# Seven half-size products for eight in the first large matmul, from the fifth block of nine on

## The chip, the cores and the metric

The kernel runs on one core of a Trainium2 chip. A core has a matrix engine (TensorE, PE in the profile; its weight loads are listed apart as PEld), a vector engine (DVE), a scalar engine (ACT), a general engine (POOL), a sync engine (SP) that here issues nearly all transfers, and 16 DMA engines. Each engine works through its own list of instructions in order and waits where an instruction needs a result of another engine. The metric is the device time of one execution in microseconds.

## The reference

```
q_s = softmax(q, axis=-1);  k_s = softmax(k, axis=2)          # q, k, v: 8 x 8 x 576 x 64
kv  = einsum('bhsd,bhse->bhde', k_s, v)
x   = einsum('bhsd,bhde->bhse', q_s, kv)  -> 4608 tokens x 512
h   = x @ w_in                                                # 512 x 2048
g   = s * maximum(h, 0)**2 + b                                # s, b: one number each
out = g @ w_out                                               # 2048 x 512
```

A linear attention gives 4608 tokens of 512 features. Two large products follow, with a squared ReLU, a scale `s` and an offset `b` between them. All arrays are float32.

## The kernel before, in words

**Blocks and steps.** The tokens form nine blocks of 512. Blocks 0 to 7 hold the first 512 tokens of one batch each; the ninth, block 8, collects the 64 left over from each batch. The 2048 hidden features are cut into 16 chunks of 128, so that a block has 16 steps and the program 144 (`step`, L738). Weights and tokens are kept split into a high and a low part, and each product is made as high x high, high x low and low x high, summed in PSUM. One step is 12 matmuls of 128 x 512 for `h` (four parts of the 512 features, three each, L726) and 12 of 128 x 512 for the output (four groups of 128 tokens, three each, L814). All of w_in and w_out stay in SBUF, in tiles called `w`, after they have been converted in block 0.

**Between the two products** stand four instructions per step: ACT takes the ReLU from PSUM (`r`, L770), DVE squares and scales (L785), ACT adds `b` and rounds to the high part `gh` (L787), DVE forms the low part `gl` (L789). Of the eight PSUM banks `h` has one and the output (`acc`) four; one called `sm` and a pair called `big` serve the attention.

**The attention of block n+1** is worked on while block n is in the two products: loads of q, k and v, maxima by way of DRAM, exponentials, a turn of q by way of DRAM (`turned`, then `qT`), the small products `kv` (L299) and `xp`, `xq` (L676), and the sum `y` of their halves (ACT L682, DVE L686). The result is rounded into the high and low parts of `x` (ACT L690, DVE L694). POOL does two large instructions for each pair of heads (L575, L592).

**What sets the order.** Every piece of work is an `Op` with an engine, a planned cost, a due number, the results it needs, and the buffers it takes and frees. A small planner (`Order.run`) goes through all streams and writes out, engine by engine, a fixed order: of the pieces that could start at nearly the same planned moment, the one with the lowest due number. On the chip each engine keeps that order.

**At a block's exit** ACT and DVE copy one half of `acc` each to SBUF and SP stores it (`leave`, L825, L828). The last block leaves in four quarters (`leave_last`, L840).

## Time and profile before

| what | value |
|---|---|
| median of 3 runs (range) | 872.04 us (871.01 to 872.32) |
| span of the profiled execution | 869.5 us |
| PE busy | 851.7 us, 98% |
| weight loads busy | 701.9 us, 81% |
| DVE busy | 570.8 us, 66% |
| ACT busy | 416.3 us, 48% |
| POOL busy | 91.4 us, 11% |
| bytes moved by DMA | 79.44 MB |

The profile is of one execution. Its span runs from the first to the last instruction; the run times are 2.5 us longer in the median (872.04 - 869.5), which is what lies around the span. Times in the timeline are microseconds from the span's start; "mean ns" is the mean duration of one instruction of a group. A matmul's recorded duration overlaps that of the next one, so its rate is read from the distance between starts. Block 1 begins at about 132 us, block 4 at about 410 us, block 7 at about 687 us; blocks 1 to 6 take some 92 us each, the attention's small products included.

### The profile page before, as it was taken

How to read it: one execution, taken by the hardware profiler on the slowest of the kernel's cores; microseconds unless marked ns; L12 is line 12 of the kernel's file. 1: busy time of each engine (PE TensorE's matmuls, PEld its weight loads, DVE VectorE, ACT ScalarE, POOL GpSimd, SP SyncE). 2: the span in 40 equal slices, each digit the busy share in tenths (PEclk: the TensorE clock that was granted, in tenths of full speed). 3: DMA queues.
4: the chain of work that ended last, by engine and by line, in shares of the span. 5: the costliest groups of instructions: out<-in, count | busy, mean ns of one | idle time of the engine just before them, and what ended most of it. 6: DMA issues, size and time to landing. Idle time of an engine off the chain costs nothing.

```text
span 869.5 us, 11637 instructions
## 1 busy us (share of the span) xinstructions
PE 851.7 (98%) x4367; PEld 701.9 (81%) x4367; DVE 570.8 (66%) x916; ACT 416.3 (48%) x694; POOL 91.4 (11%) x117
## 2 busy tenths in 40 slices
PE   7799999999999999999999999999999999999997
PEld 6578887888888888888888888888888888888886
DVE  6999997596877777686677658785855322232222
ACT  5989864544554545353545354444544322222222
POOL 1000002021102111111021202020200010000000
PEclk9999999999999999999999999999999999999999
DMA  8994134424433334342433242432311000000001
GB/s 232 308 378 136 26 86 118 127 74 97 137 82 89 83 119 100 90 92 78 130 89 83 89 130 75 96 89 82 77 61 52 33 16 1 1 30 19 1 1 48
DMA packets 109991, 79.44 MB, mean 91 GB/s; under 512 B 60656, under 2 KB 103664, under 8 KB 109808
## 3 DMA queue, kind: packets, MB, share of 16 engines
q1 hardware_dynamic: 108496, 77.60, 31.8%
q10 hardware_dynamic: 1440, 1.12, 0.4%
q8 instruction: 34, 0.56, 0.3%
q14 instruction: 21, 0.17, 0.1%
HBM read 60.29 MB, written 18.40 MB: 91 GB/s over the span
## 4 chain that ended last, share of the span: by engine, by line
PE 92%; DVE 4%; DMA 1%; SPq 1%; issue 1%; ACT 0%; ACTq 0%; DVEq 0%
PE acc L814 44%; PE h L726 44%; PE kv L299 2%; PE xp L676 1%; PE xq L676 1%; DMA k<-in_k_dram 1%; DVE low L216 1%; DMA st<-in_moe_w_in_dram 0%; DVE st L213 0%; PE xp L440 0%; DVE w L223 0%; DMA v<-in_v_dram 0%; SPq L288 0%; DVE low L206 0%; DVE st L211 0%
## 5 line engine op out<-in xcount | busy, mean ns | idle before, releaser
L726 PE MATMUL h<-x,w 128*128 128x512 f32 x1728 | 420.2, 391 | 2.4 <-ACT r L770 1.2
L726 PEld LDWEIGHTS h<-x,w 128*128 128x128 f32 x1728 | 322.7, 188 | 71.6 <-ACT r L770 1.9
L814 PE MATMUL acc<-w,gh 128*128 128x512 f32 x1152 | 357.8, 392 | 0.8 <-ACT gh L780 0.8
L814 PEld LDWEIGHTS acc<-w,gh 128*128 128x128 f32 x1152 | 214.0, 188 | 45.6 <-ACT gh L780 1.2
L785 DVE SCALAR_TENSOR_TENSOR r<-r,sb 128x512 f32<-128x512 f32 x135 | 106.1, 786 | 190.1 <-ACT r L770 189.7
L814 PE MATMUL acc<-w,gl 128*128 128x512 f32 x576 | 224.5, 390 | 0.6 <-DVE gl L782 0.6
L770 ACT ACTIVATE r<-h 128x512 f32<-128x512 f32 x143 | 85.5, 598 | 277.3 <-PE h L726 264.9
L789 DVE SCALAR_TENSOR_TENSOR gl<-r,sb,gh 128x512 fp32r<-128x512 f32 x135 | 104.5, 774 | 56.5 <-ACT gh L787 55.2
L787 ACT ACTIVATE gh<-r,sb 128x512 fp32r<-128x512 f32 x135 | 97.7, 724 | 84.8 <-DVE r L785 84.4
L814 PEld LDWEIGHTS acc<-w,gl 128*128 128x128 f32 x576 | 108.1, 188 | 23.8 <-DVE gl L782 1.1
L575 POOL TENSOR_TENSOR q<-q,qm 128x640 f32<-128x640 f32 x24 | 33.7, 1406 | 161.4 <-DVE qm L573 161.4
L592 POOL TENSOR_TENSOR qe<-qe,qr 128x640 f32<-128x640 f32 x24 | 32.3, 1347 | 65.8 <-DVE qr L588 43.7
L682 ACT COPY y<-xp 64x320 f32<-64x320 f32 x48 | 20.2, 420 | 13.8 <-PE xp L676 13.4
L686 DVE TENSOR_TENSOR y<-xp,y 64x320 f32<-64x320 f32 x48 | 23.5, 489 | 3.4 <-ACT y L682 2.5
L562 ACT ACTIVATE k<-k 128x640 f32<-128x640 f32 x24 | 17.7, 737 | 15.1 <-DVE k L524 12.3
L596 DVE STREAM_TRANSPOSE q<-qe 128x640 f32<-128x640 f32 x24 | 19.9, 831 | 5.2 <-POOL qe L592 5.2
L299 PEld LDWEIGHTS kv<-v,k 128*64 128x64 f32 x600 | 18.7, 137 | 5.1 <-issue 4.4
L656 POOL TENSOR_TENSOR spare<-kvf,spare 128x256 fp32r<-128x256 f32 x12 | 10.1, 844 | 118.6 <-issue 112.8
L613 DVE TENSOR_TENSOR qhl<-qT,qhl 64x640 fp32r<-64x640 f32 x24 | 20.6, 860 | 1.1 <-ACT qhl L610 0.4
L686 DVE TENSOR_TENSOR y<-xq,y 64x256 f32<-64x256 f32 x48 | 20.3, 422 | 1.0
L299 PE MATMUL kv<-v,k 128*64 128x65 f32 (+1 forms) x600 | 20.8, 224 | 0.0
L200 ACT ACTIVATE low<-st 128x1024 int32<-128x1024 uint32 (+1 forms) x17 | 18.9, 1111 | 3.2 <-DVE w L223 1.9
(124 smaller groups left out, 619.6 us busy)
## 6 DMA issues: line engine op xcount, KB each, us to landing
st<-in_moe_w_in_dram SPq DMA_DIRECT2D x16, 512.0 KB, 8.7
st<-in_moe_w_out_dram SPq DMA_DIRECT2D x16, 512.0 KB, 9.1
out_dram<-o SPq DMA_DIRECT2D x16, 512.0 KB, 2.7
turned<-q SPq DMA_DIRECT2D x24, 320.0 KB, 2.3
qT<-turned SPq DMA_DIRECT2D x48, 160.0 KB, 3.0
k<-in_k_dram SPq DMA_DIRECT2D x14, 512.0 KB, 4.2
q<-in_q_dram SPq DMA_DIRECT2D x14, 512.0 KB, 5.3
v<-in_v_dram SPq DMA_DIRECT2D x56, 128.0 KB, 4.8
```

The source lines that it names most:

```text
L299: nc.tensor.matmul(kv[h * D:(h + 1) * D, i], kt[:, i, h, n], vt[:, 2 * i + h, n], start=(n == 0), stop=(n == NT - 1))
L575: nc.gpsimd.tensor_tensor(out=qt, in0=qt, in1=bc(qm, [P, 2, NT, D]), op=ALU.subtract)
L592: nc.gpsimd.tensor_tensor(out=qe_, in0=qe_, in1=qr, op=ALU.mult)
L613: nc.vector.tensor_tensor(out=t[half[1 - h], h], in0=qT[half[h]], in1=t[half[h], h].bitcast(F32), op=ALU.subtract)
L682: nc.scalar.copy(y[half[h], at], parts[h][a][half[1 - h]])
L686: nc.vector.tensor_tensor(out=y[half[h], at], in0=parts[h][a][half[h]], in1=y[half[h], at], op=ALU.add)
L726: nc.tensor.matmul(hp_, w[:, j, c, :], x[:, c, :], start=(c == 0 and i == 0), stop=(c == NP - 1 and i == 2))
L770: nc.scalar.activation(r, hp_, AF.Relu)
L785: nc.vector.scalar_tensor_tensor(out=r, in0=r, scalar=s_col, in1=r, op0=ALU.mult, op1=ALU.mult)
L787: nc.scalar.activation(gh, r, AF.Identity, bias=b_col)
L789: nc.vector.scalar_tensor_tensor(out=gl, in0=r, scalar=b_col, in1=gh.bitcast(F32), op0=ALU.add, op1=ALU.subtract)
L814: nc.tensor.matmul(acc[blk, j // 2][:, j % 2], g[:, js], w_, start=(f == 0 and i == 0), stop=(f == NFC - 1 and i == 2))
```

## The change

From block 4 on (`PLAIN = 4`), the first product is made for two chunks of hidden features at a time (a pair; 40 pairs in five blocks). Weights of a pair form a 2 x 2 array of halves: two chunks (A1., A2.) by two halves of the 512 input features. The tokens form one too: two halves of the features by two halves of 256 tokens (B11, B12, B21, B22). The product of the two arrays takes eight half-size products; here it is made of seven, of sums and differences:

```
S1 = A21 + A22   S3 = A11 - A21   S2 = S1 - A11   S4 = A12 - S2
T1 = B12 - B11   T3 = B22 - B12   T2 = B22 - T1   T4 = B21 - T2
order:  P0 = A11 B11   P1 = S1 T1   P2 = A22 T4   P3 = S2 T2   P4 = S3 T3   P5 = A12 B21   P6 = S4 B22
second chunk row:  P2 + u3,  P1 + u3      with u1 = P0, u2 = P0 + P3, u3 = P0 + P3 + P4
first chunk row:   P5 + u1,  P1 + P6 + u2
```

- Each half-size product is six matmuls of 128 x 256 (L976). All seven are summed in two PSUM banks, `hset` (four quarters of 256 columns); P0, P3 and P4 follow one another in one quarter, and ACT copies the quarter out after each (u1, u2, u3, L1024). So P3 waits for the copy u1, P4 for u2, P5 for u3, P6 for the DVE sum of the second row (L1027), and the next pair's P0 for the DVE sum of the first row (L1038).
- The seven weight arrays of each pair are formed once, in blocks 1 to 3, from the converted w_in (`combine`: DVE and POOL sums, ACT and POOL splits), and stored in DRAM (14.7 MB written). In blocks 4 to 8 they are read back for every block, two products to a transfer of 512 KB, 140 transfers (`stream`, L912). The room comes from the w_in tiles, set free in block 3.
- The tokens' arrays T1 to T4 and their splits are formed per block when `x` is ready (`prepare`), for block 4 to 8.
- Between the products there are now, per pair, for one row ReLU, square and rounding on ACT and the low part on DVE; for the other one DVE instruction for ReLU and square (L997), rounding on ACT, low part on POOL (L1014).
- In blocks 4 to 7 `s` and `b` enter at the exit: out = s (r^2 w_out) + b (column sums of w_out). POOL adds up the 16 tiles of w_out in 30 additions, one pair of PE matmuls spreads the sums (`column_sums`), and both halves leave by way of DVE (L1173). Block 8 keeps `s` and `b` in the rows.
- The small products for blocks 5 to 7 take the one bank `h` in two turns in place of `big`, which `hset` holds.
- The planner gets other due numbers, and a cost added to DVE work while POOL works.

In the diff, cut:

```diff
+    DUE_S = (15.5, 13.5, 61.0, 51.0, 93.0, 76.0, 121.0, 150.5)
+    DUE_B = (33.5, 38.5, 39.5, 55.0, 37.5, 41.0, 57.5, 91.0, 95.0, 88.0, 115.0, 85.5)
+    PLAIN, FOLD = 4, 4
+    HP, OPS = NFC // 2, 7
+    KEPT = 6
...
+        else:
             for h in range(2):
+                yield Op("PE", 0.29, due - NFC, needs=needs, take=["h", "sm"], gives=[f"xp{u}"] * h, late=WAIT)
...
+    ORDER = ("A11", "S1", "A22", "S2", "S3", "A12", "S4")
+    WITH = {"A11": "B11", "S1": "T1", "A22": "T4", "S2": "T2", "S3": "T3", "A12": "B21", "S4": "B22"}
...
+    def stream(m):
...
+        yield Op("SP", 0.65, NFC * blk + 2 * uses[0][0] + DUE_ST, needs=needs, take=["pc", "ahead"], kb=512, gives=[f"s{m}"])
+        W[m] = slot()
+        nc.sync.dma_start(W[m].bitcast(F32), ws[n].rearrange("p o l e -> p o (l e)"))
...
+    def products(p):
...
+        before = {
+            0: [f"row1 {p - 1}", f"o{t - 3} {NQ - 1}"], 1: [], 2: [], 3: [f"u1 {p}"], 4: [f"u2 {p}"], 5: [f"u3 {p}"], 6: [f"row2 {p}"]
+        }
...
+        where = (1, 3, 2, 1, 1, 0, 3)
+        for k, name in enumerate(ORDER):
...
+            out_ = hset[0][:, where[k] * M:(where[k] + 1) * M]
+            w = W[m][:, j].rearrange("p (l c e) -> p l c e", l=2, c=2)
+            n = 0
+            for kt in range(2):
+                xs = x_of(blk, x, kt)
+                for a, b_ in ((0, 0), (0, 1), (1, 0)):
+                    nc.tensor.matmul(out_, w[:, a, kt], xs[:, b_], start=k < 2 and n == 0, stop=n == 5, skip_group_check=True)
+                    n += 1
...
+    def rows_a(p):
...
+        for n, k in enumerate((0, 3, 4)):
+            yield Op("ACT", 0.38, due, needs=[f"P{k} {p}"], late=LAG, near=SOON[0], gives=[f"u{n + 1} {p}"])
+            V, U = raw["V"][p % 2], raw["U"]
+            nc.scalar.copy(U if n == 2 else V[:, n * M:(n + 1) * M], hset[0][:, M:2 * M])
+        yield Op("DVE", 0.74, due, needs=[f"P2 {p}"], late=LAG, near=SOON[1], take=["r"], gives=[f"row2 {p}"])
...
-            + [step(t) for t in range(NSTEP)]
+            + [step(t) for t in range(PLAIN * NFC)]
+            + [late_(), column_sums()] + [g(i) for g in (keep_parts, combine) for i in range(HP)] + [release(f) for f in range(NFC)] + [streams()]
+            + [g(p) for p in range(NPAIR) for g in (products, rows_a, rows_b)] + [outputs(t) for t in range(PLAIN * NFC, NSTEP)]
```

**PE, two steps late in block 8.** Before, one `h` chunk of twelve matmuls and the twelve of the output of the chunk before:

```order
L726 MATMUL h_140_7075<-x_8_6142,w_12_1022 128x512 x12
L814 MATMUL acc_8_0_6734<-w_11_984,gh_139_7060 128x512 x2
L814 MATMUL acc_8_0_6734<-w_11_984,gl_139_7061 128x512
L814 MATMUL acc_8_0_6734<-w_11_984,gh_139_7060 128x512 x2
L814 MATMUL acc_8_0_6734<-w_11_984,gl_139_7061 128x512
L814 MATMUL acc_8_2_6746<-w_11_984,gh_139_7060 128x512 x2
L814 MATMUL acc_8_2_6746<-w_11_984,gl_139_7061 128x512
L814 MATMUL acc_8_2_6746<-w_11_984,gh_139_7060 128x512 x2
L814 MATMUL acc_8_2_6746<-w_11_984,gl_139_7061 128x512
L726 MATMUL h_141_7107<-x_8_6142,w_13_1085 128x512 x12
```

Now, in the last pair: P0 and P1 (two rows each), P2 (the row of six), P3, six output matmuls, P4, six output matmuls; P5, P6 and the rest of the output follow. The `w_`, `slots` names are tiles that now hold token arrays, streamed weights or `g`:

```order
L976 MATMUL hset_4051<-w_0_293,w_8_782 128x256 x3
L976 MATMUL hset_4051<-w_1_480,w_8_782 128x256 x3
L976 MATMUL hset_4051<-w_0_293,slots_4029 128x256 x3
L976 MATMUL hset_4051<-w_1_480,slots_4029 128x256 x3
L976 MATMUL hset_4051<-w_6_668,slots_4029 128x256 x6
L976 MATMUL hset_4051<-w_9_861,w_15_1280 128x256 x3
L976 MATMUL hset_4051<-w_10_887,w_15_1280 128x256 x3
L1157 MATMUL acc_8_0_7723<-w_12_1022,w_13_1085 128x512 x6
L976 MATMUL hset_4051<-w_9_861,w_15_1280 128x256 x3
L976 MATMUL hset_4051<-w_10_887,w_15_1280 128x256 x3
L1157 MATMUL acc_8_2_7738<-w_12_1022,w_13_1085 128x512 x6
```

Six output matmuls stand between P3 and P4 and again between P4 and P5; between P0 and P3 stand only P1 and P2.

**DVE in block 5.** Before, at the turn from block 4 to 5, the two instructions per step stand among those of the attention (`qhl`, `spare`, `z`):

```order
L785 SCALAR_TENSOR_TENSOR r_80_4635<-r_80_4635,sb_88 128x512
L613 TENSOR_TENSOR spare_1379<-qT_25_4574,spare_1379 64x640 x2
L825 COPY o_4_1_4663<-acc_4_2_3913 128x1024
L789 SCALAR_TENSOR_TENSOR gl_80_4637<-r_80_4635,sb_88,gh_80_4636 128x512
L785 SCALAR_TENSOR_TENSOR r_81_4694<-r_81_4694,sb_88 128x512
```

Now, in the middle of block 5, the two row sums (L1027, L1038) for which PE waits stand among them:

```order
L544 TENSOR_TENSOR k0_90<-k0_90,mb_13_5401 128x640 x2
L1027 TENSOR_TENSOR row_88_5562<-hset_4051,late_3196 128x2x4x64
L659 TENSOR_SCALAR z_13_5595<-kv_13_5564 128x2
L660 RECIPROCAL z_13_5595<-z_13_5595 128x2
L666 TENSOR_TENSOR kvf1_84<-kv_13_5564,z_13_5595 64x2x64 x4
L1038 TENSOR_TENSOR late_3196<-hset_4051,late_3196 128x2x4x64
L1014 TENSOR_TENSOR gl_1_4033<-row_88_5562,gh_1_4032 128x512
L997 SCALAR_TENSOR_TENSOR late_3196<-late_3196 128x512
L632 TENSOR_TENSOR qhl_1378<-qT_26_5484,qhl_1378 64x640 x2
```

Before, no DVE result stood between one `h` chunk's matmuls and the next one's but by way of the output; now P6 and the next P0 each wait for one.

**SP in block 5.** Before, the queue held the attention's transfers and the output; now the streamed weights (L912) stand among them, in one queue:

```order
L912 DMA w_14_1144<-ws_9_1863 128x1024
L912 DMA w_8_782<-ws_10_2082 128x1024
L1180 DMA out_0_dram<-o_4_0_5162 128x1024
L1180 DMA out_0_dram<-o_4_1_5173 128x1024
L912 DMA w_11_984<-ws_11_2101 128x1024
L912 DMA slots_4029<-ws_12_2400 128x1024
L912 DMA w_15_1280<-ws_13_2084 128x1024
L529 DMA maxima_13_5302<-top_13_5284 128x4x2
L912 DMA w_1_480<-ws_14_2331 128x1024
L912 DMA w_2_516<-ws_15_2343 128x1024
L618 DMA turned_26_5390<-q0_91 128x2x320
```

Each streamed transfer waits for a free tile, and the attention's transfers behind it in the queue wait with it.

395 lines of the change are left out of this document (337 added, 58 removed).

## The prediction

> **What bounds the kernel now.** First the page: engine shares, and the chain that ended last.
>
> ```profile
> span 869.5 us, 11637 instructions
> PE 851.7 (98%) x4367; PEld 701.9 (81%) x4367; DVE 570.8 (66%) x916; ACT 416.3 (48%) x694; POOL 91.4 (11%) x117
> GB/s 232 308 378 136 26 86 118 127 74 97 137 82 89 83 119 100 90 92 78 130 89 83 89 130 75 96 89 82 77 61 52 33 16 1 1 30 19 1 1 48
> PE 92%; DVE 4%; DMA 1%; SPq 1%; issue 1%; ACT 0%; ACTq 0%; DVEq 0%
> ```
>
> PE is busy for 98% of the span and makes up 92% of the chain (the GB/s row, in 40 slices, serves the transfers below). Averages hide stages, so next the view by windows (us, then busy time of PE, weight loads, DVE, ACT, POOL, then granted clock, DMA share, GB/s): the start, two windows in the blocks that the change touches while attention is still made, and one after it.
>
> ```profile
> 0.00:30.00 30.00, 22.28 (x207) 18.58 (x208) 22.11 (x41) 20.28 (x45) 3.80 (x21) 1.00 0.93 272
> 430.00:520.00 90.00, 90.00 (x472) 74.59 (x471) 64.08 (x109) 41.82 (x73) 13.91 (x14) 1.00 0.34 93
> 520.00:610.00 90.00, 90.00 (x470) 74.52 (x469) 64.92 (x110) 41.70 (x72) 13.62 (x14) 1.00 0.32 89
> 700.00:780.00 80.00, 80.00 (x355) 66.24 (x354) 22.28 (x29) 21.92 (x34) 4.06 (x3) 1.00 0.00 1
> ```
>
> From block 4 on PE has no idle time at full clock, and DVE, ACT and DMA have room. So every microsecond of PE work taken out there comes off the end, unless a new wait takes its place. What the PE work is, by groups (count, busy us, mean ns):
>
> ```profile
> L726 PE MATMUL h<-x,w 128*128 128x512 f32 x1728 | 420.2, 391 | 2.4 <-ACT r L770 1.2
> L814 PE MATMUL acc<-w,gh 128*128 128x512 f32 x1152 | 357.8, 392 | 0.8 <-ACT gh L780 0.8
> L814 PE MATMUL acc<-w,gl 128*128 128x512 f32 x576 | 224.5, 390 | 0.6 <-DVE gl L782 0.6
> ```
>
> Durations overlap here, so rates must come from starts, in the timeline (start, duration, engine, line, count). PE's rows around the small products of block 4, and around the last `h` chunk:
>
> ```profile
> 468.24 0.31 PE L676 MATMUL xp<-qhl,spare 128*128 128x320 f32 x1
> 468.39 0.28 PE L676 MATMUL xq<-qhl,spare 128*128 128x256 f32 x1
> 468.51 0.31 PE L676 MATMUL xp<-qhl,spare 128*128 128x320 f32 x1
> 468.65 0.28 PE L676 MATMUL xq<-qhl,spare 128*128 128x256 f32 x1
> 468.77 0.39 PE L814 MATMUL acc<-w,gh 128*128 128x512 f32 x1
> ...
> 856.06 2.88 PE L726 MATMUL h<-x,w 128*128 128x512 f32 x12
> 858.78 0.39 PE L814 MATMUL acc<-w,gh 128*128 128x512 f32 x1
> ```
>
> Twelve full-size matmuls take 858.78 - 856.06 = 2.72 us, 0.2267 us each. Half-size ones (256 columns, each with its own weight load) take 468.51 - 468.39 = 0.12 and 468.77 - 468.65 = 0.12. Finer: the four take 0.53 us for 1152 columns; with 0.2267 for 512 that makes 0.42 ns a column and 0.011 us a matmul, so 0.119 us for 256. A half costs 52% of a whole.
>
> **The change, part by part.** *PE.* Removed: blocks 4 to 8 had 5 x 16 x 12 = 960 full-size `h` matmuls, 960 x 0.2267 = 217.6 us. Added: 40 pairs x 7 x 6 = 1680 half-size ones, 1680 x 0.119 = 199.9 us. Net **-17.7 us**, 0.44 per pair. The rounding of the rows allows 0.116 to 0.121: -22.7 to -14.3. In the trace half-size matmuls alternate with longer ones, in the change 42 weight loads come with 42 half-size matmuls nearly in a row. Can loads keep up? The rows of the transposes, which load 128 x 128 each and stream only 128 columns:
>
> ```profile
> 29.77 0.92 PE L440 MATMUL xp<-early,kvf 128*128 128x256 f32 x3
> 30.52 0.71 PE L430 MATMUL qT<-ident,qe 128*128 128x128 f32 x5
> ...
> L430 PE MATMUL qT<-ident,qe 128*128 128x128 f32 x40 | 5.7, 274 | 0.2 <-DVE qe L426 0.2
> ...
> L440 PE MATMUL xp<-early,kvf x32: 377/432/483, 19.9 to 134.8; 128*128 128x256 f32 x16, 128*128 128x320 f32 x16
> ```
>
> Five take 0.71 us, the last 0.274 of it: (0.71 - 0.27) / 4 = 0.11 us from load to load. That is under 0.119, so loads still hide, barely. The break-even is (217.6 - 1.8) / 1680 = 0.128 us per half-size matmul.
>
> *Column sums on PE.* Two plain float32 products of 512 columns. Of such products the first row above has three instructions in 30.52 - 29.77 = 0.75 us (one of 256 columns, two of 320), 0.84 ns a column. Each product is recorded twice (32 rows of L440 for 16 in the program), so two of 512 columns are 4 x 512 x 0.84 = 1.7; **+1.8 us** with the hand-over. The 30 POOL additions ahead of them have all of block 3.
>
> *The waits inside a pair* are the new risk. The rows that price them:
>
> ```profile
> 858.98 0.66 ACT L757 ACTIVATE r<-h 128x256 f32<-128x256 f32 x2 [3.30 <-PE h L726]
> 862.38 0.59 ACT L840 COPY last<-acc 128x512 f32<-128x512 f32 x1 [1.55 <-PE acc L814]
> 863.01 0.19 PEld L814 LDWEIGHTS acc<-w,gh 128*128 128x128 f32 x1 [0.42 <-ACT last L840]
> ...
> L682 ACT COPY y<-xq 64x256 f32<-64x256 f32 x48 | 17.6, 367 | 0.9
> L686 DVE TENSOR_TENSOR y<-xp,y 64x320 f32<-64x320 f32 x48 | 23.5, 489 | 3.4 <-ACT y L682 2.5
> L686 DVE TENSOR_TENSOR y<-xq,y 64x256 f32<-64x256 f32 x48 | 20.3, 422 | 1.0
> ```
>
> ACT started 0.20 us after PE went on to other work (858.98 against 858.78); PE started 0.04 after ACT's end (862.97 to 863.01). A quarter's copy is 0.37. So u1, u2, u3 take 0.20 + 0.37 + 0.04 = 0.61 us each. By PE's new order P0 to P3 is covered by P1 and P2 (12 x 0.119 = 1.43), P3 to P4 and P4 to P5 by six output matmuls (1.36). A row sum of 512 columns is an estimate from L686: 67 ns per 64 columns more, 0.69 us. P4 to P6 takes copy, sum and three hand-overs, 0.20 + 0.37 + 0.05 + 0.69 + 0.04 = 1.35, cover 1.36 + 0.71 = 2.07; P6 to the next P0 0.93, cover 2.72. With engines free nothing waits. In blocks 7 and 8 they are free: DVE 22.28 of 80 us.
>
> In blocks 4 to 6 foreign work stands in front. DVE: 64.08 per 90 us is 65.8 per block of 92.4; less 16 steps of L785 and L789, plus the new rows:
>
> ```profile
> L785 DVE SCALAR_TENSOR_TENSOR r<-r,sb 128x512 f32<-128x512 f32 x135 | 106.1, 786 | 190.1 <-ACT r L770 189.7
> L789 DVE SCALAR_TENSOR_TENSOR gl<-r,sb,gh 128x512 fp32r<-128x512 f32 x135 | 104.5, 774 | 56.5 <-ACT gh L787 55.2
> L782 DVE TENSOR_TENSOR gl<-r,gh 128x512 fp32r<-128x512 f32 x8 | 5.5, 692 | 2.2 <-ACT gh L780 2.2
> L770 ACT ACTIVATE r<-h 128x512 f32<-128x512 f32 x143 | 85.5, 598 | 277.3 <-PE h L726 264.9
> L787 ACT ACTIVATE gh<-r,sb 128x512 fp32r<-128x512 f32 x135 | 97.7, 724 | 84.8 <-DVE r L785 84.4
> L613 DVE TENSOR_TENSOR qhl<-qT,qhl 64x640 fp32r<-64x640 f32 x24 | 20.6, 860 | 1.1 <-ACT qhl L610 0.4
> L712 POOL TENSOR_TENSOR x<-xleft_all,x 128x512 fp32r<-128x512 f32 x4 | 5.4, 1338 | 72.5 <-ACT x L710 72.5
> L694 DVE TENSOR_TENSOR x<-y,x x24: 628/684/1752, 179.6 to 666.0; 128x512 fp32r<-128x512 f32 x24
> ```
>
> 65.8 - 25.0 = 40.8; plus 8 pairs x (2 x 0.69 + 0.786 + 0.692) = 22.9; plus token arrays (six of 0.42, five of 0.69, 6.0, less four L694 of 0.84, 3.4) 2.6; plus the exit's other half 1.2: 67.5 of a block of 88.9, 76% against 71%. So the engine is no bound, but one attention instruction (0.86, L613) in front of a row sum makes it 2.21 against a cover of 2.07; two make it 3.07. (An ACT instruction of 0.72 in front of u2 makes 1.33, still covered.) Below: nothing. Above: 0.8 us, one instruction too many, in each of 24 pairs, 19 us. I take 0.1 per pair, **+2.4 us**, near the lower end, since DVE is free a quarter of the time and one foreign instruction costs 0.14.
>
> *POOL* gets 8 low parts and three splits per block, 11 x 1.338 = 14.7 us, and DVE feels POOL: L694 takes 0.684 in the median and 1.752 at most. The Trainium skill ("SBUF — State Buffer", "SBUF: two separate sides") says of the port pair that DVE and GpSimd share that it is an exclusive lock, the loser waiting out the whole instruction. The 1.752 agrees; by it 14.7 us more would be lost to DVE per block, 82 of 88.9 us by my estimate.
>
> *Blocks 1 to 3* get the weight sums: DVE 16 x 0.69 + 16 x 0.42 = 17.8 us in 277, POOL 46 x 1.338 and 16 of half that, 72 us, the column sums included. There an `h` chunk's way to the output has 24 matmuls of cover (5.44 us) for 0.598 + 0.786 + 0.724 + 0.774 = 2.9 us and four hand-overs: nothing. *The end:* after the last P6 stand 24 output matmuls, 5.44 us, before chunk 15's; its row needs 0.93 + 0.79 + two ACT instructions like L787 (1.45) + POOL 1.34, 4.5. Nothing.
>
> *Transfers.* 28 x 0.524 = 14.7 MB per block of 88.9 us, 165 GB/s, beside 93: 258 GB/s. The first window had 272 at a share of 0.93, its third slice 378. Six transfers are held ahead, twelve products, over 15 us, against:
>
> ```profile
> st<-in_moe_w_in_dram SPq DMA_DIRECT2D x16, 512.0 KB, 8.7
> qT<-turned SPq DMA_DIRECT2D x48, 160.0 KB, 3.0
> ```
>
> The stream is covered even at 8.7 us. The attention's own round trips, behind it in SP's queue, may come later: 0 to 8 us in three blocks; I take none.
>
> **Sum.** 869.5 - 17.7 + 1.8 + 2.4 = 856.0 for a profiled span; the median of the runs lies 2.5 above the span: **858.5 us**.
>
> **Rivals.**
> *Attention comes late.* PE's list has 24 halves of `xp` and 6 `kv` for blocks 5 to 7 in it, each now needing `sm`, `h` and DRAM round trips. If the busier queue (3.0 to 8.7 us landing) delays 6 turns of q by what the cover doesn't hold, 6 x 1.3 = 8 us: 866.5. For: the share of 0.93 in the first window. Against: the 378 GB/s of the third slice, so 258 is no ceiling.
> *Row sums behind stretched attention work, slower than before.* Place: P6 and P0 in blocks 4 to 6. Price: a row sum behind one L613 (0.86) and one POOL stretch (1.752 - 0.684 = 1.07) needs 1.35 + 1.93 = 3.28 against 2.07, 1.2 us in each of 24 pairs, 29 us: 885. It decides from (17.7 - 1.8) / 24 = 0.66 us per pair. For: 76% on an engine that works in order. Against: the stretch is the extreme of 24.
> *A half-size matmul costs more than half.* If each had to show a part of its 0.188 us load and cost three quarters of a whole, 0.170 us, then 1680 x 0.170 = 285.6, +68 in place of -17.7: 944. Against: the 0.12 and the 0.11. The Trainium skill ("TensorE: Matmul & The Clock Gate", "Back-to-back issue gap") gives a sustained 81 ns for 128 columns and 131 for 512; by a line through these, an estimate, a half is three quarters of a whole. The trace's 0.2267 and 0.119 disagree with both.
> *No stalls at all* and 0.1175 per matmul: 853.
>
> **How the numbers follow.** Forecast 0.60, late attention 0.18, slower by row sums 0.08, dear half-size 0.02, no stalls 0.12. The first reaches from 855 to 862; with the two neighbours 852 to 868 holds some 85 in 100. A change under 0.2% can't be told from none: 870.3 to 873.8 counts as the same, chance 0.03; slower 0.09 (the two rivals less what falls short of the point, and the tail); faster 0.88.
>
> **What would show it.** `hset` matmuls 0.117 to 0.121 us from start to start, blocks 7 and 8 some 3.5 us shorter than 87 and PE without idle: the first term. Idle of PE before `hset` by DVE or ACT over 5 us in blocks 4 to 6: the row sums. Idle before `xp` or `kv` with the turn of q late: the transfers. I am wrong if `hset` matmuls stand 0.125 us or more apart, or if blocks 1 to 3 grow.

## The result and the profile after

The changed kernel takes **917.64 us** (median of 4 runs, 915.16 to 918.19) against 872.18 us (871.01 to 872.97): ratio 1.0515, 95% interval 1.05 to 1.0531. Forecast were 858.5 us, 852 to 868. It is slower by 45 us where 14 us less were forecast; of the two rivals on the slower side the row sums had 885 and the dear half-size matmuls 944. The profiled execution has a span of 913.4 us in a time of 915.16 (the lowest of the four); the ledger below is made on spans.

The page of the changed kernel: the span, the busy time of the engines, the shares of the chain that ended last (the work and waits followed back from the last instruction).

```profile
span 913.4 us, 13898 instructions
PE 863.1 (94%) x5091; PEld 725.4 (79%) x5091; DVE 641.1 (70%) x989; ACT 483.4 (53%) x881; POOL 246.0 (27%) x230
PE 71%; DVE 15%; issue 4%; ACT 4%; SPq 2%; DMA 2%; POOL 1%; DVEq 0%; ACTq 0%; POOLq 0%
```

PE fell from 98% to 94% of the span and from 92% to 71% of the chain; DVE's share of the chain rose from 4% to 15%. So PE now waits. Where, the windows tell, cut at the first `h` or `hset` matmul of each block (us, busy time of PE, weight loads, DVE, ACT, POOL, then granted clock, which is the share of TensorE's full rate that it had in that stretch, DMA share, GB/s). Before, blocks 1 to 3, and block 7:

```profile
131.90:225.60 93.70, 93.69 (x485) 77.34 (x485) 71.44 (x120) 47.20 (x81) 17.42 (x17) 1.00 0.37 95
225.60:318.00 92.40, 92.40 (x482) 76.59 (x481) 68.72 (x117) 43.88 (x77) 14.58 (x15) 1.00 0.38 105
318.00:410.30 92.30, 92.30 (x481) 76.52 (x480) 68.71 (x116) 44.66 (x78) 13.84 (x16) 1.00 0.37 96
...
687.40:774.50 87.10, 87.10 (x386) 72.11 (x385) 26.52 (x34) 24.12 (x37) 5.35 (x4) 1.00 0.03 13
```

After, blocks 1 to 7:

```profile
131.70:226.30 94.60, 94.03 (x485) 77.28 (x486) 73.56 (x120) 47.65 (x81) 26.53 (x25) 1.00 0.56 152
226.30:323.10 96.80, 93.87 (x483) 76.17 (x482) 88.08 (x139) 48.85 (x89) 40.66 (x35) 1.00 0.62 171
323.10:432.10 109.00, 98.93 (x482) 77.42 (x481) 101.81 (x132) 48.05 (x88) 70.16 (x51) 0.97 0.43 124
432.10:527.10 95.00, 90.98 (x618) 79.44 (x617) 69.14 (x120) 53.28 (x109) 26.69 (x24) 1.00 0.84 253
527.10:625.00 97.90, 92.87 (x626) 80.91 (x625) 70.17 (x119) 50.89 (x107) 27.45 (x25) 1.00 0.79 234
625.00:721.20 96.20, 92.46 (x625) 80.74 (x624) 60.69 (x103) 50.41 (x105) 23.70 (x22) 1.00 0.70 222
721.20:811.80 90.60, 86.91 (x529) 76.09 (x528) 30.34 (x45) 34.16 (x68) 14.19 (x12) 1.00 0.54 187
```

Two losses of different kinds stand in these rows. Block 3, which the change gives no new product, takes 109.0 us for 92.3, with DVE busy for 101.8 of them and POOL for 70.2. PE is idle for 10.1 us there; the other 6.6 are busy time, 98.9 for 92.3 us at nearly the same number of matmuls (482 and 481): ahead of a stop a matmul counts with its whole 0.39 us, where otherwise the next one starts after 0.2267. And block 7, where DVE is busy for 30 of 90 us and nothing of attention is left, takes 90.6 for 87.1 where 3.5 less were forecast: PE has 3.7 us idle there. What ended PE's idle times (us in total, times, longest):

```profile
PE hset L976 <- ACT late L1024: 18.6, 40, 1.0
PE acc L1157 <- DVE gl L1132: 6.1, 8, 1.9
...
PE hset L976 <- DVE row L1027: 1.4, 6, 0.6
```

The first row is the key to blocks 4 to 8: there are 40 pairs, and PE waits 40 times for ACT's copy of a quarter, once in every pair. The forecast had that copy covered.

The time from the first product of each block to that of the next, for all kernels of this study (us; "8 and end" runs to the span's end):

| kernel | block 1 | 2 | 3 | 4 | 5 | 6 | 7 | 8 and end |
|---|---|---|---|---|---|---|---|---|
| before | 93.7 | 92.4 | 92.3 | 92.4 | 92.3 | 92.4 | 87.1 | 95.0 |
| after | 94.6 | 96.8 | 109.0 | 95.0 | 97.9 | 96.2 | 90.6 | 101.6 |
| two_tiles | 94.6 | 98.4 | 108.8 | 88.5 | 89.4 | 89.5 | 84.3 | 95.2 |
| told | 94.6 | 99.6 | 108.6 | 96.1 | 107.5 | 90.3 | 87.7 | 98.9 |
| few_sums | 94.6 | 98.4 | 98.1 | 95.6 | 97.5 | 97.1 | 90.5 | 101.5 |
| pe_sums | 94.6 | 98.4 | 141.6 | 106.7 | 105.2 | 95.7 | 90.6 | 101.5 |
| pe_sums_once | 94.6 | 98.4 | 103.1 | 92.1 | 98.0 | 96.2 | 90.6 | 101.4 |
| b_over_s | 94.6 | 98.4 | 96.5 | 86.7 | 89.4 | 89.5 | 84.3 | 95.7 |
| no_combine | 93.8 | 93.9 | 95.1 | 88.1 | 89.5 | 89.5 | 84.3 | 95.1 |
| later_combine | 93.7 | 99.5 | 93.4 | 87.7 | 89.5 | 89.4 | 84.3 | 95.5 |
| tuned_one | 93.6 | 98.2 | 93.9 | 86.7 | 89.5 | 89.5 | 84.3 | 95.2 |
| tuned_two | 99.9 | 93.4 | 94.1 | 87.2 | 89.4 | 89.5 | 84.3 | 95.6 |
| sums_behind_block_2 | 93.7 | 92.9 | 95.5 | 90.7 | 100.0 | 89.6 | 84.4 | 95.1 |

### The profile page after: what moved, and what is told of

It reads as the page before. It is cut to its first block, busy times and chain, and to the rows that moved or that the text cites. A ratio compares the mean times of both kernels' runs of the same rounds, so it can differ in the third digit from the quotient of the medians.

```text
span 913.4 us, 13898 instructions
## 1 busy us (share of the span) xinstructions
PE 863.1 (94%) x5091; PEld 725.4 (79%) x5091; DVE 641.1 (70%) x989; ACT 483.4 (53%) x881; POOL 246.0 (27%) x230
## 4 chain that ended last, share of the span: by engine, by line
PE 71%; DVE 15%; issue 4%; ACT 4%; SPq 2%; DMA 2%; POOL 1%; DVEq 0%; ACTq 0%; POOLq 0%
PE acc L1157 34%; PE hset L976 23%; PE h L1068 10%; DVE gl L1132 3%; PE kv L319 2%; ACT late L1024 2%; DVE y L686 2%; DVE r L1128 2%; DMA st<-in_moe_w_out_dram 1%; DVE qs L601 1%; DVE x L743 1%; DVE q L615 1%; SPq L299 1%; DVE row L1027 1%; DMA k<-in_k_dram 1%
## 5 line engine op out<-in xcount | busy, mean ns | idle before, releaser
L1157 PE MATMUL acc<-w,gh 128*128 128x512 f32 x936 | 294.1, 396 | 3.3 <-ACT gh L1130 2.5
L1068 PE MATMUL h<-x,w 128*128 128x512 f32 x768 | 190.6, 393 | 5.7 <-ACT r L1113 2.8
L1068 PEld LDWEIGHTS h<-x,w 128*128 128x128 f32 x768 | 142.5, 188 | 39.2 <-ACT r L1113 4.3
L976 PE MATMUL hset<-w,w 128*128 128x256 f32 x1032 | 154.3, 286 | 11.1 <-ACT late L1024 10.9
L976 PEld LDWEIGHTS hset<-w,w 128*128 128x128 f32 x1032 | 137.9, 191 | 24.2 <-ACT late L1024 15.3
L1024 ACT COPY late<-hset 128x256 f32<-128x256 f32 x120 | 44.6, 372 | 155.5 <-PE hset L976 154.4
L1027 DVE TENSOR_TENSOR row<-hset,late 128x512 f32<-128x512 f32 x40 | 27.7, 691 | 124.4 <-ACT late L1024 116.2
L1014 POOL TENSOR_TENSOR gl<-late,gh 128x512 fp32r<-128x512 f32 x26 | 35.1, 1351 | 197.5 <-ACT gh L1012 183.3
L1157 PE MATMUL acc<-w,w 128*128 128x512 f32 x300 | 76.3, 393 | 0.0
L1130 ACT ACTIVATE gh<-r,sb 128x512 fp32r<-128x512 f32 x56 | 40.5, 723 | 45.0 <-DVE r L1128 44.7
L1157 PEld LDWEIGHTS acc<-w,w 128*128 128x128 f32 x300 | 53.6, 189 | 9.9 <-ACT last L1210 0.4
L1038 DVE TENSOR_TENSOR late<-hset,late 128x512 f32<-128x512 f32 x40 | 27.6, 690 | 46.8 <-PE hset L976 46.5
L1128 DVE SCALAR_TENSOR_TENSOR r<-r,sb 128x512 f32<-128x512 f32 x56 | 50.1, 894 | 11.8 <-ACT r L1113 11.3
L1132 DVE SCALAR_TENSOR_TENSOR gl<-r,sb,gh 128x512 fp32r<-128x512 f32 x56 | 51.8, 926 | 7.0 <-ACT gh L1130 6.2
L976 PE MATMUL hset<-slots,w 128*128 128x256 f32 x288 | 51.0, 290 | 5.0 <-ACT late L1024 3.9
L976 PEld LDWEIGHTS hset<-slots,w 128*128 128x128 f32 x288 | 41.3, 190 | 11.5 <-ACT late L1024 5.7
L976 PE MATMUL hset<-w,slots 128*128 128x256 f32 x312 | 46.0, 286 | 3.6 <-ACT late L1024 3.4
L976 PEld LDWEIGHTS hset<-w,slots 128*128 128x128 f32 x312 | 41.2, 191 | 7.8 <-ACT late L1024 5.1
```

The source lines that it names most:

```text
L976: nc.tensor.matmul(out_, w[:, a, kt], xs[:, b_], start=k < 2 and n == 0, stop=n == 5, skip_group_check=True)
L1014: by(eng).tensor_tensor(out=gl, in0=row, in1=gh.bitcast(F32), op=ALU.subtract)
L1024: nc.scalar.copy(U if n == 2 else V[:, n * M:(n + 1) * M], hset[0][:, M:2 * M])
L1027: nc.vector.tensor_tensor(out=by_token(row, blk), in0=as_token(both(hset[0][:, 2 * M:4 * M]), blk), in1=as_token(U.unsqueeze(1).to_broadca ...
L1038: nc.vector.tensor_tensor(out=by_token(row, blk), in0=as_token(hset[0].rearrange("p (a b) -> p a b", a=4)[:, 0:4:3], blk), in1=as_token(bo ...
L1068: nc.tensor.matmul(hp_, w[:, j, c, :], x[:, c, :], start=(c == 0 and i == 0), stop=(c == NP - 1 and i == 2))
```

## The experiments

Two theories. **A**: in each pair PE stops before P2, because the copy u1 of P0 is held until P1 is done, though P1 writes another quarter; the cause is that `hset` is one tile for whoever sets the waits. Its rival: ACT comes late by its own queue. **B**: blocks 1 to 3 pay for POOL's additions, which slow DVE's steps. Its rival: they pay for DVE's own new instructions, or for something else of the preparation.

### A: one tile or two (two_tiles, told)

The edit of two_tiles, cut to its core:

```diff
-                hset.append(ps.tile([P, 2, 512], F32, name="hset", tag="big").rearrange("p a b -> p (a b)"))
-            out_ = hset[0][:, where[k] * M:(where[k] + 1) * M]
+                hset.extend(ps.tile([P, 512], F32, name=f"hset{c}", tag=tag, bufs=1) for c, tag in enumerate(("h", "sm")))
+            out_ = hset[where[k] // 2][:, where[k] % 2 * M:(where[k] % 2 + 1) * M]
...
-                yield Op("PE", 0.29, due - NFC, needs=needs, take=["h", "sm"], gives=[f"xp{u}"] * h, late=WAIT)
+                yield Op("PE", 0.29, due - NFC, needs=needs, take=["big"], gives=[f"xp{u}"] * h, late=WAIT)
```

> The partial products of a pair in blocks 4 to 8 stand in two tiles of one bank each (quarters 0 and 1, quarters 2 and 3) instead of one tile of two banks; the small products of attention in blocks 5 to 7 take the two-bank tile that this frees; the sum of the first row takes two instructions of 256 columns instead of one of 512. Theory A (u1, the copy of P0, waits for P1 only because P1 writes another quarter of the same tile, and P2 then waits for u1): the copy starts behind P0, P1 and P2 cover it, PE's stop of 0.62 us in each of 40 pairs goes: 917.6 - 24.8 = 893 us, 889 to 899; idle of PE before hset put down to ACT falls from 18.6 us to under 5. Rival (ACT reaches u1 late by its own queue, whatever tile it reads): the stop moves from P2 to P3 and the time stays at 910 to 920.

Measured: **883.09 us** (882.52 to 883.35), ratio to before 1.0124 (1.0109 to 1.014). That is 34.5 under the changed kernel, more than the 24.8 expected. Nothing of `hset` is left among PE's waits. First the pair as it was, in the timeline of the changed kernel (start, duration, engine, line, count, in brackets the idle time ahead and who ended it):

```profile
857.14 1.59 PE L976 MATMUL hset<-w,w 128*128 128x256 f32 x12
...
858.77 0.37 ACT L1024 COPY late<-hset 128x256 f32<-128x256 f32 x1 [1.19 <-PE hset L976]
859.19 1.70 PE L976 MATMUL hset<-w,w 128*128 128x256 f32 x12 [0.46 <-ACT late L1024]
860.73 0.63 PE L1157 MATMUL acc<-w,w 128*128 128x512 f32 x2
```

P0 and P1 are the first row. P0 alone would be done after 6 x 0.12 = 0.72 us, at 857.9; u1 starts at 858.77, behind P1. ACT had been idle for 1.19 us and waited for PE, so its queue is not to blame. Then P2 waits for u1. With two tiles:

```profile
744.11 1.59 PE L982 MATMUL hset<-w,w 128*128 128x256 f32 x12
745.02 0.37 ACT L1030 COPY late<-hset 128x256 f32<-128x256 f32 x1 [1.18 <-PE hset L982]
745.54 0.88 PE L982 MATMUL hset<-w,slots 128*128 128x256 f32 x6
...
746.26 0.52 PE L982 MATMUL hset<-slots 128*128 128x256 f32 x3
746.62 0.52 PE L982 MATMUL hset<-w,slots 128*128 128x256 f32 x3
746.98 0.63 PE L1165 MATMUL acc<-w,gh 128*128 128x512 f32 x2
```

u1 starts 0.91 us after P0's start, inside P1, and P0 to P3 take 746.98 - 744.11 = 2.87 us for 24 matmuls, 0.1196 each, against 860.73 - 857.14 = 3.59. That is 0.72 us a pair, 28.8 us in 40 pairs; my 24.8 had counted only the gap of 0.62 ahead of P2's first matmul. From block 4 to the end the kernel gained 481.3 - 446.9 = 34.4 us of span, which is 5.6 beyond the 28.8. A part of the 5.6 lies at P5, which with one tile waits for the second row's sum: P5 and P6 take 854.39 - 852.89 = 1.50 us in the changed kernel and 825.68 - 824.25 = 1.43 with two tiles. In block 7, where there is no attention, a pair gains (90.6 - 84.3) / 8 = 0.79 us, 31.5 in 40 pairs; the 2.9 that are left of the 34.4 lie in blocks 4 to 6 (the six waits for the second row's sum, 1.4 us, are among them) and were not split further. The cause shows in the program too, in the list of PE's instructions with what each waits for (tile names shortened). P0 and P2 of a pair of the changed kernel (in this pair P1 waits for nothing, nor does P3):

```
L976 MATMUL hset<-w_734,slots 128x256 [waits DMAHW2_49,DVE_49]
L976 MATMUL hset<-slots,w_605 128x256 [waits DMAHW3_49,Activation_49]
```

and P2, P3 of a pair of two_tiles:

```
L982 MATMUL hset_4052<-w_887,w_605 128x256 [waits DMAHW5_49]
L982 MATMUL hset_4051<-w_861,w_605 128x256 [waits Activation_49]
```

The wait for ACT has gone from P2 to P3, where the sums need it: of the 40 pairs, P2 waits for ACT in 38 in the changed kernel and in none with two tiles, P3 in 2 and in all 40.

The second run of this theory keeps the one tile and puts the waits that it has into the plan:

```diff
-            0: [f"row1 {p - 1}", f"o{t - 3} {NQ - 1}"], 1: [], 2: [], 3: [f"u1 {p}"], 4: [f"u2 {p}"], 5: [f"u3 {p}"], 6: [f"row2 {p}"]
+            0: [f"row1 {p - 1}", f"o{t - 3} {NQ - 1}"], 1: [], 2: [f"u1 {p}"], 3: [], 4: [f"u2 {p}"], 5: [f"u3 {p}", f"row2 {p}"], 6: []
...
-        for n, k in enumerate((0, 3, 4)):
+        for n, k in enumerate((1, 3, 4)):
```

> One tile as in the changed kernel, but the order of the work is planned with the waits that the built program has: u1 needs P1, P2 needs u1, P5 needs the second row's sum; output products then stand between P1 and P2. Theory A: the same 24.8 us go, without any other tile, 893 us, 889 to 901. Rival (u1 late by ACT's queue): the output products cover that wait too, so this one alone falls and two tiles doesn't. If the stop were the price of a change of output quarter on PE, neither falls.

Measured: **914.53 us** (913.82 to 917.34), ratio 1.0483 (1.0466 to 1.0501): 3 us of the 24.8. PE's waits of this kernel:

```profile
PE hset L976 <- DVE late L1038: 7.4, 23, 1.8
PE acc L1157 <- DVE gl L1132: 6.6, 9, 1.9
PE xp L726 <- DVE y L686: 4.2, 3, 3.6
...
PE hset L976 <- ACT late L1024: 2.3, 4, 1.2
```

The stop at u1 did go, from 18.6 us to 2.3. That alone does not decide between the readings, since by the rival the output products would cover a late ACT too. What decides against the rival is the run with two tiles, together with the 1.19 us for which ACT waited for PE; and a price of changing the output quarter falls with the same run, where the products change quarters in the same order. But the time hardly fell: `hset` now waits for the first row's sum (L1038) 23 times, 7.4 us, and blocks 4 and 5 became longer (96.1 and 107.5), while 6 to 8 became shorter. A pair has 24 output products, 5.44 us, to put between its parts; with one tile there is a fourth place that needs them, and my expectation took cover for free. This is not all of block 5: the longest of its waits are those of `xp` for a sum of the attention (4.1 us) and of the output for a copy at the exit (2.4), at a granted clock of 0.94, and why the new order leads to them was not traced. The two tiles take the wait away, the plan for the most part moved it.

### B: the column sums (few_sums, pe_sums, pe_sums_once)

```diff
-        for f in range(1, NFC):
+        for f in range(1, 2):
             for i in range(2):
                 yield Op("POOL", 1.4, DUE_C, needs=["late"])
```

> 28 of the 30 additions of the column sums on POOL are left out (b is then multiplied by the sums of the first two 128-row pieces of w_out alone, so that part of the output is left out); all else as in the changed kernel. Theory B (POOL's additions slow DVE's steps, 0.35 us of DVE for each us of POOL, and block 3's h chunks wait for gl): 28 x 1.73 = 48 us of POOL, 17 us of DVE, and of block 3's 16.7 us more some 13 go: 904 us, 900 to 909. Rival (DVE's own new instructions, the weight sums, are what blocks 2 and 3 pay): under 4 us, 914 to 918.

Measured: **907.22 us** (906.57 to 908.35), ratio 1.0403 (1.0388 to 1.0419): 10.4 us less. Block 3 fell from 109.0 to 98.1. DVE's work there is the same, and only POOL's is less. What that does to DVE shows in the groups of block 3 (busy us and mean ns of one). Before the change:

```profile
L789 DVE SCALAR_TENSOR_TENSOR gl<-r,sb,gh 128x512 fp32r<-128x512 f32 x17 | 12.7, 745 | 5.2 <-ACT gh L787 5.0
L686 DVE TENSOR_TENSOR y<-xp,y 64x320 f32<-64x320 f32 x8 | 3.9, 489 | 0.5 <-ACT y L682 0.3
```

After it:

```profile
L1132 DVE SCALAR_TENSOR_TENSOR gl<-r,sb,gh 128x512 fp32r<-128x512 f32 x16 | 19.4, 1213 | 1.4 <-ACT gh L1130 1.2
L686 DVE TENSOR_TENSOR y<-xp,y 64x320 f32<-64x320 f32 x10 | 4.9, 488 | 0.2
L1189 POOL TENSOR_TENSOR late<-late,w 128x512 f32<-128x512 f32 x28 | 43.6, 1582 | 0.2
```

And with few_sums:

```profile
L1132 DVE SCALAR_TENSOR_TENSOR gl<-r,sb,gh 128x512 fp32r<-128x512 f32 x16 | 14.1, 884 | 2.4 <-ACT gh L1130 2.3
```

The same step of an `h` chunk takes 745, 1213 and 884 ns as POOL is busy for 13.8 of 92.3, 70.2 of 109.0 and 26.5 of 98.1 us. The sum of L686, whose first input is in PSUM, stays at 488. An instruction that came at a random moment and waited for the end of POOL's current one would lose 70.16 / 109.0 x 1.58 / 2 = 0.51 us in the mean, 1255 ns; measured 1213. The rule by which the forecast was weighed (the Trainium skill, "SBUF — State Buffer", "SBUF: two separate sides": the pair of ports that DVE and GpSimd share is locked for a whole instruction, for DVE when it has two inputs in SBUF) agrees with both numbers, the 1213 and the 488. Single instructions show it more plainly. One `gl` of block 3 after the change, with POOL's instruction ahead of it and the matmul behind it:

```profile
399.42 1.33 POOL L675 TENSOR_TENSOR spare<-kvf,spare 128x256 fp32r<-128x256 f32 x1
400.17 1.12 DVE L1132 SCALAR_TENSOR_TENSOR gl<-r,sb,gh 128x512 fp32r<-128x512 f32 x1
...
401.35 0.50 PE L1157 MATMUL acc<-w,gl 128*128 128x512 f32 x1 [0.17 <-DVE gl L1132]
```

POOL ends at 400.75 and `gl` at 401.29. Of the 16 `gl` in this block eleven start while POOL is at an instruction, and each ends 0.55 us after that instruction's end, however much of it was left; the other five take 653 to 753 ns. Before the change none of the 17 met more than a memset of POOL's.

The next run does the same sums on PE:

```diff
...
+        for f in range(NFC):
+            yield Op("PE", 0.46, DUE_C, take=() if f else ["sm"])
+            sums = sums or ps.tile([P, 512], F32, name="sums", tag="sm", bufs=1)
+            for i in range(2):
+                nc.tensor.matmul(sums, one, wo[f][:, i], start=f == 0 and i == 0, stop=f == NFC - 1 and i == 1)
         yield Op("ACT", 0.6, DUE_C, free=["sm"], gives=["bias"])
...
+        raw["bias"] = raw["F"][:, 0]
+        nc.scalar.activation(raw["bias"], sums, AF.Copy, scale=b_col)
```

> The column sums by 32 full-size matmuls of PE with ones, and b as the scale of the copy that follows; no additions on POOL. PE pays 32 x 0.2267 = 7.3 us, less the 1.8 us of the two plain float32 products: +5.5. Theory B: 904 + 5.5 = 909.5, 905 to 914, block 3 some 9 us shorter than 109. Rival (DVE's own instructions): 917.6 + 5.5 = 923.

Measured: **968.03 us** (967.32 to 969.09), ratio 1.11 (1.1084 to 1.1117), 58 us over what theory B expected and 45 over its rival. Neither had the reason. PE's waits in block 3:

```profile
PE kv L319 <- ACT k L581: 16.6, 1, 16.6
PE xp L708 <- POOL spare L675: 6.1, 2, 3.1
...
PE kv L319 <- ACT late L1196: 0.8, 1, 0.8
```

The 16 steps were due last of all, and from the first of them on they held the one-bank tile `sm`: the first of the 32 matmuls starts at 333.3 us, the last at 424.7. The `kv` products of block 4's attention need that tile. The first of them starts at 425.9, as soon as ACT has copied the sums out (L1196, the last row); the 16.6 us stand before the second, whose `k` ACT then made late. So urgent work stood behind work that the plan put off. The test of this reading makes the 32 products one step:

```diff
+        yield Op("PE", 7.3, DUE_C, take=["sm"])
+        sums = ps.tile([P, 512], F32, name="sums", tag="sm", bufs=1)
         for f in range(NFC):
-            yield Op("PE", 0.46, DUE_C, take=() if f else ["sm"])
-            sums = sums or ps.tile([P, 512], F32, name="sums", tag="sm", bufs=1)
```

> The column sums on PE again, on the changed kernel with one tile, but as one piece of work of 7.3 us in the plan instead of 16 pieces due last of all. If pe_sums lost its 50 us because the 16 pieces held the one-bank tile that block 4's attention needed (PE then stood 16.6 us before a kv product), this one has what pe_sums was expected to have: 909.5 us, 905 to 914. If PE's products with ones cost more than 0.2267 us each or the granted clock falls with them, it stays over 920.

Measured: **908.39 us** (906.39 to 910.11), ratio 1.0418 (1.0398 to 1.0438), 1 us from the 909.5 expected. Block 3 is at 103.1, of which 7.3 are the products. The first of these starts at 332.3 us, the last at 339.5, and the first `kv` product follows at 341.1. So the sums on PE cost no more than their 32 matmuls, and the 60 us between the two runs are the order alone.

### B without sums at all, and A with it (b_over_s)

The algebra allows the column sums to be dropped: s(r² + b/s) needs b/s where `gh` is rounded, and the exit's s.

```diff
-    G_ON = ('DVE', 'POOL')
+    G_ON = ('DVE', 'DVE')
...
-        nc.scalar.copy(gh, row)
...
-        by(eng).tensor_tensor(out=gl, in0=row, in1=gh.bitcast(F32), op=ALU.subtract)
...
+            nc.scalar.activation(gh, row, AF.Identity, bias=raw["bs"])
...
+            by(eng).scalar_tensor_tensor(out=gl, in0=row, scalar=raw["bs"], in1=gh.bitcast(F32), op0=ALU.add, op1=ALU.subtract)
...
-                out=o, in0=acc.pop((blk, j)), scalar=s_col, in1=raw["bias"].unsqueeze(1).to_broadcast([P, 2, DO]), op0=ALU.mult, op1=ALU.add
+            nc.vector.tensor_scalar(o, acc.pop((blk, j)), s_col, None, op0=ALU.mult)
```

> Two tiles as in the run of that name, and no column sums at all: b divided by s is added where gh is rounded (the bias of ACT's copy, the scalar of DVE's subtraction), and the exit multiplies by s; the low parts of the second rows go from POOL to DVE. The output is whole. Theory B (the additions on POOL are what block 3 pays for): 883.1 less the 10.4 us that leaving out 28 additions gave, less the 1.8 us of the two float32 products: 871 us, 867 to 875; blocks 4 to 6 stay at 89 to 90 us though DVE gets 8 x 0.77 us more in each. Rival (with the rows' low parts on DVE the row sums come late): blocks 4 to 6 at 92 us or more, 880 or above.

Measured: **869.81 us** (868.96 to 870.87), ratio 0.9978 (0.9969 to 0.9988): at the expected 871, and the first version that is not slower than before. Its windows, blocks 3 and 5, and 7:

```profile
325.70:422.20 96.50, 94.22 (x481) 75.99 (x480) 79.05 (x136) 49.61 (x90) 22.90 (x22) 1.00 0.52 153
...
508.90:598.30 89.40, 89.40 (x625) 80.80 (x624) 72.61 (x134) 52.88 (x106) 16.20 (x16) 1.00 0.85 258
...
687.80:772.10 84.30, 84.30 (x530) 76.26 (x529) 37.63 (x62) 35.77 (x68) 4.42 (x3) 1.00 0.56 196
```

PE has no idle time in block 5, though DVE works for 72.6 of 89.4 us, 81%. The rival (row sums late with all low parts on DVE) is out.

### B: the weight sums (no_combine, later_combine, tuned_one, tuned_two, sums_behind_block_2)

no_combine is two_tiles with the edit of few_sums, and with this in place of the combination:

```diff
-            nc.vector.tensor_tensor(out=F[:, j], in0=w[:, 0], in1=w[:, 1], op=ALU.add)
...
-            by(S_ON[n]).tensor_tensor(out=out_, in0=x, in1=y, op=op)
...
-            by(S_ON[4 + j]).tensor_tensor(out=t[:, 1], in0=F[:, j], in1=t[:, 0].bitcast(F32), op=ALU.subtract)
+            nc.scalar.copy(t[:, 0], w_tile(g)[:, 0].bitcast(F32))
...
+            nc.scalar.copy(t[:, 1], w_tile(g)[:, 1].bitcast(F32))
```

> Two tiles, 28 of the 30 column additions left out as in few_sums, and the combination of w_in left out too: DVE and POOL make no sums of its quarters, ACT copies plain pieces in their place, so that all stores, loads and products stand (the output of blocks 4 to 8 is not the reference's). Theory B: what is left of the loss in blocks 1 to 3 (13 us in few_sums: 94.6, 98.4 and 98.1 us against 93.7, 92.4 and 92.3) is this work on DVE and POOL; it goes, blocks 2 and 3 fall to 92 to 94 us, and the run comes to 883.1 - 10.4 - 11 = 862, 858 to 866. Rival (the stores and gates on the SP queue, or the half-size stage itself): blocks 1 to 3 stay, 870 to 874.

Measured: **863.47 us** (863.12 to 864.24), ratio 0.9905 (0.989 to 0.992), expected 862. Blocks 1 to 3, windows:

```profile
132.60:226.40 93.80, 93.75 (x485) 77.37 (x486) 67.53 (x113) 53.19 (x95) 15.21 (x15) 1.00 0.60 171
226.40:320.30 93.90, 92.93 (x482) 76.39 (x481) 73.16 (x120) 52.89 (x94) 20.04 (x19) 1.00 0.61 177
320.30:415.40 95.10, 94.67 (x485) 77.11 (x484) 75.09 (x126) 47.16 (x86) 18.41 (x19) 1.00 0.48 135
```

The stores, the gates and their queue stay, and the blocks are within 4.4 us of before (282.8 against 278.4). With few_sums, which differs by the weight sums and the two tiles, they are 291.1; two tiles alone do not shorten these blocks (301.8 with two_tiles, 300.4 in the changed kernel). So the weight sums on DVE and POOL, 8.3 us, are the other part of the loss in blocks 1 to 3. What the 4.4 us that stay are was not tested.

Is it their work or their place? later_combine changes two rows of numbers in b_over_s:

```diff
-    DUE_S = (15.5, 13.5, 61.0, 51.0, 93.0, 76.0, 121.0, 150.5)
+    DUE_S = (150, 150, 150, 150, 150, 150, 150, 150)
...
-    GATE = (21, 23, 25, 29, 33, 37, 41, 43)
+    GATE = (17, 22, 27, 32, 37, 42, 47, 52)
```

> b_over_s with the weight sums moved only: each pair's combination may begin after h chunk 17, 22, 27, 32, 37, 42, 47, 52 instead of 21, 23, 25, 29, 33, 37, 41, 43, and it comes last in the choice of ACT, DVE and POOL (due 150 for all eight). No instruction is added or removed. Theory B, sharper (block 2 loses its 6 us because the sums stand in front of the attention that makes block 2's x, not because DVE is full): block 2 falls from 98.4 us towards 94, the rest stays: 869.8 - 4 = 866, 863 to 868. Rival (the work itself is the price wherever it stands): 869 to 872.

Measured: **866.83 us** (866.39 to 867.37), ratio 0.9942 (0.9928 to 0.9957). The total was as expected, the place wasn't: block 2 stays at 99.5, blocks 1 and 3 lose 0.9 and 3.1. So the agreement of the total is luck, and coming last in the choice did not help block 2; the first three gates (17, 22, 27) still lie in block 1, whose chunks are 16 to 31. Two further sets of the plan's numbers were tried on it. The edit of the first, tuned_one, to later_combine, in the main:

```diff
-    X_ON = ('POOL', 'DVE', 'POOL', 'DVE', 'POOL', 'DVE')
+    X_ON = ('POOL', 'POOL', 'POOL', 'DVE', 'POOL', 'DVE')
...
-    DUE_R = (-41.5, -60.5)
+    DUE_R = (-71.5, -60.5)
...
-    GATE = (17, 22, 27, 32, 37, 42, 47, 52)
+    GATE = (17, 22, 27, 32, 37, 42, 52, 53)
...
-    DUE_ST = -20.0
+    DUE_ST = -4.0
```

> later_combine with a handful of the plan's numbers moved further: last two gates at 52 and 53, the first rows' row work due earlier, one low part of the token arrays from DVE to POOL, streams due later. By the theory that foreign work in front of rows and of x is all that is left: 1 to 4 us below later_combine, 862 to 866. Rival: no change, since blocks 4 to 8 have no idle of PE left to take out.

Measured: **865.6 us** (865.43 to 865.67), ratio 0.9928 (0.9911 to 0.9944), 1.2 under later_combine and the fastest kernel here that computes everything.

The second, tuned_two, sets the plan's durations to the profile's and has numbers chosen for them:

```diff
-    GATE = (17, 22, 27, 32, 37, 42, 52, 53)
+    GATE = (16, 22, 27, 32, 37, 49, 52, 52)
...
-    def on(eng, pool=1.4, dve=0.77):
+    def on(eng, pool=1.73, dve=0.74):
...
-            yield Op("DVE", 0.66, due, two=True)
+            yield Op("DVE", 0.78, due, two=True)
```

> As tuned_one, but the plan's durations are set to what the profile shows (POOL's low part 1.73 for 1.40 us, DVE's two steps per h chunk 0.78 for 0.66, ACT's 0.60 and 0.72 for 0.50 and 0.62), and its numbers are chosen for these. If the plan's durations being too short is what makes blocks 1 to 3 longer than planned: under 864. If the order they lead to is no better (blocks 1 and 2 planned longer): 866 to 870.

Measured: **867.97 us** (866.8 to 868.58), ratio 0.9954 (0.9939 to 0.9968). Durations nearer to the profile's, with the numbers chosen for them, did not give a better order; block 1 became 99.9 us long. The second of the two readings holds for this set, in which nine rows of numbers differ from tuned_one's.

What is left in block 2, tuned_one's waits in that block show:

```profile
PE h L1081 <- ACT x L747: 1.7, 1, 1.7
PE h L1081 <- DVE x L749: 1.0, 1, 1.0
```

Block 2's own first `h` chunk waits for the last quarter of its `x`. The last run puts all weight sums behind that point, by the gates alone:

```diff
-    GATE = (17, 22, 27, 32, 37, 42, 52, 53)
+    GATE = (34, 36, 39, 42, 45, 48, 51, 54)
```

> tuned_one with all gates of the weight sums behind the start of block 2 (h chunks 34, 36, 39, 42, 45, 48, 51, 54), nothing else changed: in block 1 no weight sum stands beside the attention that makes block 2's x. If these sums are what makes that x late (PE stops at block 2's first h chunk and runs at a granted clock of 0.5 to 0.6 behind the stops): block 2 falls from 98.2 us to 93 or 94; the work then crowds blocks 3 to 5, so the whole may well be longer than 865.6 (870 to 880). Rival (block 2's x is late by its own chain of round trips): block 2 stays at 97 us or more.

Measured: **876.34 us** (875.17 to 877.39), ratio 1.0056 (1.004 to 1.0073). Block 2 falls to 92.9 us, and the waits above are gone: PE is idle for 0.2 us in its window. Its windows of blocks 1 and 2, nearly:

```profile
132.00:226.00 94.00, 94.00 (x488) 77.56 (x487) 69.35 (x116) 47.03 (x82) 17.33 (x16) 1.00 0.38 97
226.00:318.00 92.00, 91.80 (x478) 75.76 (x477) 76.76 (x131) 45.82 (x80) 29.62 (x28) 1.00 0.62 175
```

So weight sums in block 1 are what makes block 2's `x` late (no_combine, which keeps their stores and leaves the sums out, has block 2 at 93.9); whether by the time that they take on DVE or by POOL's effect on DVE was not split. The same work then crowds blocks 4 and 5 (90.7 and 100.0), as expected, and the whole is longer.

## Why the prediction was wrong

By its own steps.

*PE, -17.7: right.* With the waits away, P0 to P3 run at 0.1196 us a matmul, inside the 0.116 to 0.121 of the forecast, 217.6 - 1680 x 0.1196 = 16.7. Blocks 5 and 6 come to 89.4 and 89.5 for 92.3 and 92.4, block 7 to 84.3 for 87.1, about 3 us each. The doubt whether weight loads keep up was unfounded, and the rival "costs more than half" (944) with it.

*Column sums on PE, +1.8: right.* They stand in block 4: from their start to the end of the six half-size matmuls behind them are 448.71 - 446.28 = 2.43 us, less 6 x 0.1196 that is 1.7. The sentence beside it, that the 30 additions ahead of them "have all of block 3", is where 10 us went.

***The waits inside a pair, +2.4: wrong, measured 34.4.*** The step that failed is "P0 to P3 is covered by P1 and P2 (12 x 0.119 = 1.43)". Its price for u1, 0.61 us, was right: from P0's start to P2's are 859.19 - 857.14 = 2.05 us, less 12 x 0.1196 that is 0.61. Wrong was when it begins and who waits for it. I took both from the plan's table of needs, where u1 needs P0, and P3 needs u1. The built program has other waits, since it treats `hset` as one tile: u1 waits for P1, P2 for u1, and no cover stands between P1 and P2 (and P5 waits for the second row's sum, where the table has P6). The share of DVE in blocks 4 to 6, on which this part of the forecast dwelt, hardly matters (1.4 us in six waits).

***Blocks 1 to 3, nothing: wrong, measured 21.8*** (first product of block 4 at 432.1 for 410.3). The count of new work was fair for DVE's own instructions and low for POOL: 72 us against a measured 137.4 - 45.8 = 91.5 (sums of the windows above). But DVE's busy time rose by 263.5 - 208.9 = 54.6 us and not by 17.8; the 36.8 beyond are 0.40 us for each microsecond of POOL's new work. The forecast compared an `h` chunk's way, 2.9 us, with its cover of 5.44, at durations that were taken with POOL nearly idle and with DVE's queue free. It had the row for this in hand (L694, 0.684 in the median and 1.752 at most) and the rule of the lock, and applied both to blocks 4 to 6, where they cost little, and not to block 3, where POOL is busy two thirds of the time. Of the loss (300.4 us in the three blocks for 278.4) 9.3 go with 28 of the 30 column additions, 8.3 with the weight sums, and 4.4 stay open. Nor had the forecast a term for what stops cost beyond their length, 6.6 of block 3's 16.7 us. "I am wrong ... if blocks 1 to 3 grow" was the right alarm.

*The end, transfers:* as forecast. No wait for a stream is among PE's waits, at a DMA share of up to 0.84.

*The rivals.* "Row sums behind stretched attention work" had DVE's stretch by POOL as its mechanism, which is real; but the rival placed it in blocks 4 to 6, and it decided in block 3. "Attention comes late" by its round trips: not seen in blocks 5 to 7; the one late `x` is block 2's, by weight sums in front. No rival held the wait between P1 and P2.

**The ledger** of the span: 869.5 - 16.7 (PE) + 1.8 (column sums on PE) + 34.4 (pairs) + 21.8 (blocks 1 to 3) = 910.8; measured 913.4. The 2.6 us that are left lie from block 4 on (two_tiles has 446.9 there for 459.2 before, 12.3 less, where 16.7 - 1.8 make 14.9). The forecast took the output matmuls as unchanged, but in block 7 they follow one another at 230.6 ns in the mean with two_tiles, and at 226.8 before; with 192 a block that would be 3.6 us in five blocks, which is an estimate from this one block, and why they are slower stays open. The 2.5 us that the forecast added around the span are 1.8 in the executions on record (915.16 - 913.4). Two_tiles takes off the 34.4, b_over_s 12.3 of block 3, no_combine shows the weight sums at 8.3; without the three the time is near the forecast's 858.5: no_combine, which has two tiles, two of the 30 additions and no weight sums, runs in 863.5.
